# FFT filter and snake MLP on one core: the first DFT stage of batches 3 to 7 by sums and differences on GpSimd, batch 1's forward pieces half a step later, and another order of the last stores

## The chip, the cores and the metric

The kernel runs on one core of a Trainium2 chip. The metric is the time of one execution on the device in microseconds (us). Five engines work side by side, each through its own instructions in order: TensorE (PE in the profile), VectorE (DVE), ScalarE (ACT), GpSimd (POOL) and SyncE (SP), which here only issues DMAs. PEld is TensorE's loading of weights.

## The reference

```python
def _attn_ref(x, filt_r, filt_i):          # x: 8 batches, 3008 rows, 256 channels, float32
    X = np.fft.rfft(x, axis=1)
    F = (filt_r + 1j * filt_i)[None, :, :]
    return np.fft.irfft(X * F, n=x.shape[1], axis=1)

def _moe_ref(x, w_in, w_out, alpha):       # x: 24064 x 256, w_in: 256 x 2048, w_out: 2048 x 256
    h = x @ w_in
    s = np.sin(alpha * h)
    g = h + s * s / (alpha + 1e-09)
    return g @ w_out
```

The second function takes the first one's result as 24064 rows of 256. A filter in frequency over each batch's 3008 rows is followed by two matrix products with an activation between them.

## The kernel before

The transform of length 3008 = 47 x 64 is done in two stages. For each batch from 1 on the class `Spectral` holds the pieces:

- `load_x` (L141, GpSimd's queue): four loads of 94 rows x 8 x 256, fp32 cast to fp16 on the way. Each starts only after the activation that was last recorded (`after(ins, marks["snake"])`).
- `first` (L181): 16 matmuls, 94 rows of contraction (47 samples x 2 halves) by 96 outputs (24 frequencies, real and imaginary part, 2 halves) over 512 columns; `evac` copies the result from PSUM to `t1_h`, two of three times on ACT (L160), else on DVE (L162). After every fourth a store goes from `t1_h` to `d1` in DRAM (L186, SP).
- `load_t2` (L193, GpSimd's queue): eight loads that bring `d1` back turned, 64 rows x 6 x 256 each; two of them make the group of three forward pieces.
- `forward` (L201): 12 pieces of two matmuls of 256 columns; ACT copies to `xf` (L204); two DMAs on SP swap the halves into `xs` (L208).
- `product`, `cross` (L215, L221, L222): the filter, on DVE.
- `inverse` (L232) and the store of `g` to `d2` (L239, SP); `load_t4` (L244, SP); `last` (L254): the inverse's second stage into `y`.

The MLP runs over 48 chunks of 512 (some 384) columns. `hidden` makes 128 hidden units at a time: two matmuls `ph` (L541), a sine on ACT (L545), one operation on DVE (L546). `project` makes 8 matmuls `po` of 256 columns (L558); two tiles of 128 columns are copied by ACT (L566) to `o` and go out by `store` (L586) in parts, since the 94 rows of a run of `y` wrap inside a tile: 4 to 8 DMAs per pair of tiles, on GpSimd's queue up to chunk 4, then on SP. In the last chunk each of the last two tiles is copied and stored by itself, with ACT's queue as the second one.

Batch 0 is done ahead of all this by another path. From there on the order is written out by hand. `put(at, fn, ...)` files each piece under a step; a chunk has eight steps. In a step stand four `ph` matmuls (two hidden blocks), a slot for pieces due, eight `po` matmuls, and a second slot at half a step. A slot lets in one piece with matmuls, more only if it is overdue by over a step:

```python
            if pending[0][2]:
                if run and pending[0][0] > at - 1:
                    break
                run += 1
```

With z = 48 b, batch b's first stage is filed from z - 67 on (0.66 of a step apart), its t2 loads at z - 56, its first forward piece at z - 46.8; in batch 1 the forward pieces begin at step 17.5, 1.25 apart. All engines keep the order in which the pieces are let in, so a piece that waits for data holds up what stands behind it on its engine.

Of the kernel before, what the change touches and what calls it, by code (L numbers as in the profile page):

```python
# [20 lines left out]
N1, N2 = 47, 64  # L21
NS, NQ = 24, 64
NR = 2 * N1
NK = 4 * NS
FUSED = 1


def dft_tables():

    n1, n2 = np.arange(N1), np.arange(N2)  # L30
    s, q = np.arange(NS), np.arange(NQ)
    ph = 2 * np.pi * np.outer(n1, s) / N1
    w = np.stack([np.cos(ph), -np.sin(ph)], 1)
    wf = np.zeros((N1, 2, 2, NS, 2))
    wi = np.zeros((2, NS, 2, N1, 2))
    v = np.stack([2 * np.cos(ph), -2 * np.sin(ph)], 0)
    v[0, :, 0], v[1, :, 0] = 1.0, 0.0
    for h in range(2):
        wf[:, h, :, :, h] = w
        wi[:, :, h, :, h] = v.transpose(0, 2, 1) * (8.0 / S)  # L40

    kap = np.where(q[:, None] < 32, s + N1 * q[:, None], s + N1 * (95 - q[:, None]))
    sg = np.where(q < 32, 1.0, -1.0)[:, None]
    th = 2 * np.pi * n2[:, None, None] * kap / S
    c, sn = np.cos(th), np.sin(th)
    d = np.zeros((2, N2, NS, 2, NQ))
    d[0, :, :, 0] = c.transpose(0, 2, 1)
    d[1, :, :, 0] = sn.transpose(0, 2, 1)
    d[0, :, :, 1] = (-sn * sg).transpose(0, 2, 1)
    d[1, :, :, 1] = (c * sg).transpose(0, 2, 1)  # L50
    f16 = np.float16
    wf, wi = wf.reshape(N1 * 2, 2, NS, 2), 2 * wi.reshape(2, NS, 2, NR)
    wf0, wi0 = np.zeros((96, 2, 2, 32)), np.zeros((2, 2, 32, NR))
    wf0[:NR, :, :, :NS] = wf.transpose(0, 1, 3, 2)
    wi0[:, :, :NS] = wi.transpose(0, 2, 1, 3)
    d = d.reshape(128, NS, 128).astype(f16)
    e = d.transpose(2, 1, 0) * f16(0.125)
    return (wf.reshape(NR, NK).astype(f16), wi.reshape(NK, NR).astype(f16), d,
            wf0.reshape(96, 128).astype(f16), wi0.reshape(128, NR).astype(f16), e)


# [1 line left out]
def kernel(  # L63
# [8 lines left out]
    out: bass.AP,  # L72
):
    nc = tc.nc
    wf_host, wi_host, d_host, wf0_host, wi0_host, e_host = dft_tables()
    wf_dram = nc.inline_tensor(wf_host, name="wf_tbl")
    wi_dram = nc.inline_tensor(wi_host, name="wi_tbl")
    d_dram = nc.inline_tensor(d_host, name="d_tbl")
    wf0_dram = nc.inline_tensor(wf0_host, name="wf0_tbl")
    wi0_dram = nc.inline_tensor(wi0_host, name="wi0_tbl")  # L80
# [13 lines left out]
        return ctx.enter_context(tc.tile_pool(name=name, bufs=bufs, **kw))  # L94

    cpool = pool("consts", 1)
    xpool = pool("xp", 4)
    t2pool = pool("t2", 4)
    xfpool = pool("xf", 3)
    ppool = pool("pp", 4)  # L100
# [7 lines left out]
    ops = pool("ops", 2, PSUM)  # L108

    wf_t = cpool.tile([NR, NK], FP16)  # L110
    t1_h = [cpool.tile([128, 16, C], FP16, name=f"t1_h{i}") for i in range(2)]
    t4_a = cpool.tile([128, 2, 16, C], FP16)
    t4_h = [t4_a[:, i] for i in range(2)]

    def by_half(t):

        return t.rearrange("p a (b c) -> p (a b) c", c=128)

    cos_all = cpool.tile([128, 4, 512], FP32)
    y = cpool.tile([128, 2, 2, 32, NR], FP16)  # L120
# [15 lines left out]
    marks = {}  # L136

    def load_x(b, ch):
        xt = xpool.tile([NR, 8, C], FP16, name=f"x_{b}_{ch}", tag="x")
        for n0, n in [(0, 8)] if b or ch < 3 else [(0, 4), (4, 4)]:  # L140
            ins = nc.gpsimd.dma_start(  # L141
                out=xt[:, n0:n0 + n],
# [14 lines left out]
    def evac(dst, src, on_act=None):  # L157
# [3 lines left out]
        else:  # L161
            marks["dve"] = nc.vector.tensor_copy(out=dst, in_=src)  # L162

    class Spectral:

        def __init__(self, b):
            self.b = b
            self.d1 = dpool.tile([2 * NS, N2, C], FP16, name=f"d1_{b}", tag="d1")
            self.d2 = dpool.tile([2 * NS, N2, C], FP16, name=f"d2_{b}", tag="d2")
            self.d1_rows = self.d1.rearrange("a (h n) c -> (a h) n c", h=2)  # L170
            self.d2_rows = self.d2.rearrange("a (h n) c -> (a h) n c", h=2)
            self.x, self.t2, self.t4, self.xf, self.xs, self.p = {}, {}, {}, {}, {}, {}
            self.fused = b >= FUSED

        def load_x(self, ch):
# [2 lines left out]
        def first(self, i):  # L178
# [6 lines left out]
            if j == 3:  # L185
                nc.sync.dma_start(out=self.d1_rows[:, 8 * ch:8 * ch + 8, :],   # L186
                                  in_=t1_h[ch // 2][0:NK, r0:r0 + 8, :])

        def load_t2(self, g):
            self.t2[g] = t2pool.tile([128, 6, C], FP16, name=f"t2_{self.b}_{g}", tag="t2")  # L190
# [73 lines left out]
    id32 = cpool.tile([16, 16], FP32)  # L264
    nc.scalar.dma_start(out=id32, in_=id32_dram.ap())

    x0 = [xpool.tile([NR, 8, C], FP16, name="x_0_0", tag="x")] + [load_x(0, ch) for ch in range(1, 4)]
    nc.gpsimd.dma_start(out=d_t, in_=d_dram.ap())
    id16 = cpool.tile([128, 128], FP16)
    nc.gpsimd.dma_start(out=id16, in_=id16_dram.ap())  # L270
# [166 lines left out]

    def product_0(i):
        hc, w = blocks[i]
        p0[i] = xpool.tile([128, 2, 4, 128], FP16, name=f"p_0_{i}", tag="x")  # L440
        marks["products"] = nc.vector.tensor_tensor(
            out=p0[i].rearrange("p f s (k c) -> p f s k c", k=2),
            in0=xf0[i].rearrange("p s (k c) -> p s k c", k=2)[:, None].to_broadcast([128, 2, 4, 2, 64]),
# [27 lines left out]
        marks["w_in"] = ins  # L471
    nc.sync.dma_start(out=wf_t, in_=wf_dram.ap())
    nc.sync.dma_start(out=wi_t, in_=wi_dram.ap())
    w_out32 = vpool.tile([128, 16, C], FP32, name="w_out32", tag="v")
    for jb in range(0, 16, 8):
        ins = nc.sync.dma_start(out=w_out32[:, jb:jb + 8],
# [73 lines left out]
    def project(k, u):  # L550

        pb, c0, n = chunks[k]
        t, half = divmod(u, 2)
        final = k == len(chunks) - 1 and t > 1
        if (t % 2 == 0 or final) and half == 0:
            pso[k] = ops.tile([128, 2, C], FP32, name=f"po_{k}_{t}", tag="o")
        for jb in range(8 * half, 8 * half + 8):
# [5 lines left out]
        if half == 1 and (t % 2 == 1 or last or final):  # L563
# [2 lines left out]
            nc.scalar.copy(out=o[:, i0:t % 2 + 1, :], in_=pso[k][:, i0:t % 2 + 1, :])  # L566
            for i in range(i0, t % 2 + 1):
                store(o[:, i, :], pb, c0 + 128 * (t - t % 2 + i),
                      nc.scalar if final else nc.gpsimd if k < 5 or k == len(chunks) - 1 else nc.sync, k < 5)

    def runs(cnt):

        whole = cnt if max(d for d in range(1, 17) if cnt % d == 0) > 7 else cnt - cnt % 16
        return [(0, whole), (whole, cnt - whole)] if 0 < whole < cnt else [(0, cnt)]

    def store(o_blk, pb, col, second, alone):

        p = 0
        queues = [second if alone else nc.sync, second]
        while p < 128:  # L580
            odd, rest = divmod(col + p, S)
            n2, row = divmod(rest, NR)
            cnt = min(128 - p, NR - row)
            t0 = (2 * pb + odd) * S + 32 * row + n2
            for i, (r0, rows) in enumerate(runs(cnt)):
                queues[i].dma_start(  # L586
                    out=bass.AP(tensor=out.tensor, offset=out.offset + (t0 + 32 * r0) * C,
                                ap=[[32 * C, rows], [1, C]]),
                    in_=o_blk[p + r0:p + r0 + rows, :])
            p += cnt  # L590

    pending = []

# [8 lines left out]
    for b in range(1, B):  # L602
        s = s1 if b == 1 else Spectral(b)
        z = 48 * b
        if b > 1:
            for ch in range(4):
                put(22 + 4 * ch if b == 2 else z - 92 + 7 * ch, s.load_x, ch)
        for i in range(16):
            put(6.9 + 0.35 * i if b == 1 else 37 + 0.63 * i if b == 2 else z - 67 + 0.66 * i, s.first, i, pe=True)
        for g in range(4):  # L610
            put(12.5 if b == 1 else 47 if b == 2 else z - 56, s.load_t2, g)
        for u in range(12):
            inv = 23.5 + 1.25 * u if b == 1 else 59 + 2.1 * u if b == 2 else z - 40.8 + 2.3 * u
            fwd = inv - (6 if b == 1 else 6)
            put(fwd, s.forward, u, pe=True)
            put(fwd + (0.5 if b == 1 else 1.5), s.product, u)
            if s.fused:
                put(fwd + (4 if b == 1 else 4.5), s.cross, u)
            put(inv, s.inverse, u, pe=True)
        for ch in range(4):  # L620
            put(z - (9.5 if b == 1 and ch < 3 else (10.5, 10.5, 10.5, 3)[ch]), s.load_t4, ch)
        for u in range(16):
# [60 lines left out]
```

## Time and profile before

| What | Value |
|---|---|
| Time, median of 3 runs | 785.33 us (783.27, 785.33, 3184.2) |
| The profiled execution | 786.9 us, span of its instructions 785.0 us |
| Granted TensorE clock | 1.000 |
| TensorE busy | 773.5 us, 99% of the span |
| DVE, ACT, GpSimd busy | 652.8, 617.7, 113.1 us |
| First stage `first` (L181) | 112 matmuls |
| DMA | 100.99 MB, mean 129 GB/s |

The span is the time from the first to the last instruction; 1.9 us of the profiled execution lie around it. Matmuls overlap, so TensorE's busy time and the mean of one matmul say more than one more matmul costs; the chain of waits gives the time from one start to the next. The columns of a group are: line, engine, operation, output<-inputs, shape, count | busy us, mean ns of one | idle us before them and what ended it. A line of the timeline or of the chain begins with the start and the length in us; a q behind an engine's name is its queue of instructions, which issues DMAs. A line of the waits gives the time in all, how often, and the longest.

### The profile page before, as it was taken

The page shows a single profiled execution, that of the slowest core. Times are in us where ns is not written, and L with a number is a line of the kernel's source. Part 1 is how long each engine was busy: PE and PEld are TensorE (multiplying, and loading weights), DVE is VectorE, ACT ScalarE, POOL GpSimd, SP SyncE. Part 2 cuts the span into 40 slices and gives each one's busy share as a digit, 9 for nine tenths or more (in the row PEclk, how much of TensorE's full clock was granted, in tenths as well). Part 3 has the DMA queues.
Part 4 walks back from the last instruction along what each step waited for, and adds up shares of the span by engine and source line. Part 5 has one row for each costly group of instructions (what it writes and reads, how often), then busy time and mean ns, then how long its engine had stood idle before and what let it go on. Part 6 is the DMA issues. An engine that isn't in the chain of part 4 may idle for free.

```text
span 785.0 us, 16642 instructions
## 1 busy us (share of the span) xinstructions
PE 773.5 (99%) x5799; PEld 535.6 (68%) x5799; DVE 652.8 (83%) x1163; ACT 617.7 (79%) x1213; POOL 113.1 (14%) x190
## 2 busy tenths in 40 slices
PE   8998999999999999999999999999999999999998
PEld 4756767676677666777667776767667776766666
DVE  6886997899878997799878998789987899777773
ACT  5797988888878887888878888788787887777674
POOL 6356544400020000200020000200002000000000
PEclk9999999999999999999999999999999999999999
DMA  9955586665664546654574454835456233421111
GB/s 215 276 111 153 115 184 193 155 127 121 171 166 85 129 104 194 145 124 107 128 210 107 104 115 131 227 87 124 114 159 177 65 98 78 119 62 28 41 41 54
DMA packets 86655, 100.99 MB, mean 129 GB/s; under 512 B 14896, under 2 KB 74294, under 8 KB 86572
## 3 DMA queue, kind: packets, MB, share of 16 engines
q1 hardware_dynamic: 74644, 71.11, 32.7%
q0 software_dynamic: 11712, 28.78, 18.5%
q8 instruction: 45, 0.74, 0.4%
q14 instruction: 38, 0.31, 0.1%
q10 hardware_dynamic: 216, 0.05, 0.0%
HBM read 55.72 MB, written 46.66 MB: 130 GB/s over the span
## 4 chain that ended last, share of the span: by engine, by line
PE 93%; DVE 3%; DMA 2%; ACT 1%; issue 1%; SPq 0%; POOL 0%; ACTq 0%; DVEq 0%; POOLq 0%
PE po L558 40%; PE ph L541 40%; PE pa L181 3%; PE pb L201 2%; PE pd L254 2%; PE pc L232 2%; DVE v L546 1%; PE pc L453 1%; DMA al<-in_moe_alpha_dram 1%; PE warm L377 1%; DMA d<-t_h 1%; PE pb L431 1%; DMA t<-d 0%; PE pa L399 0%; SPq L586 0%
## 5 line engine op out<-in xcount | busy, mean ns | idle before, releaser
L546 DVE SCALAR_TENSOR_TENSOR v<-cos_all,ph 128x512 f16<-128x512 f32 (+1 forms) x768 | 483.1, 671 | 110.9 <-ACT cos_all L545 107.7
L545 ACT ACTIVATE cos_all<-ph 128x512 f32<-128x512 f32 (+1 forms) x768 | 411.2, 592 | 94.1 <-PE ph L541 93.2
L558 PE MATMUL po<-w,v 128*128 128x256 f16 x3008 | 389.3, 272 | 0.0
L541 PE MATMUL ph<-y,w 128*128 128x512 f16 (+1 forms) x1536 | 387.8, 374 | 0.7 <-DVE v L546 0.6
L558 PEld LDWEIGHTS <-v 128*128 128x128 f16 x3008 | 288.3, 98 | 77.9 <-issue 1.5
L541 PEld LDWEIGHTS <-w 128*128 128x128 f16 x1536 | 147.9, 98 | 103.8 <-issue 3.3
L566 ACT COPY o<-po 128x512 f32<-128x512 f32 (+1 forms) x97 | 55.7, 574 | 20.7 <-PE po L558 14.3
L586 POOL DMA_DIRECT2D out_dram<-o x67 | 34.8, 528 | 208.3 <-ACT o L566 207.4
L204 ACT CAST xf<-pb 128x512 f16<-128x512 f32 x84 | 49.9, 594 | 14.7 <-PE pb L201 13.1
L193 POOL DMA_DIRECT2D t<-d x56 | 36.3, 663 | 172.7 <-DMA out_dram<-o 96.7
L141 POOL DMA_DIRECT2D x<-in_x_dram x32 | 17.2, 539 | 266.6 <-PE pc L232 160.0
L160 ACT CAST t_h<-pa 96x512 f16<-96x512 f32 x77 | 45.0, 584 | 8.4 <-PE pa L181 8.2
L160 ACT CAST y<-pd 128x376 f16<-128x376 f32 (+1 forms) x83 | 39.9, 480 | 8.2 <-PE pd L254 4.4
L254 PEld LDWEIGHTS <-t_a 96*128 96x128 f16 x448 | 31.4, 97 | 18.6 <-issue 0.4
L181 PE MATMUL pa<-x,wf_t 94*96 94x512 f16 x112 | 42.5, 381 | 0.7 <-ACT t_h L160 0.4
L160 ACT CAST g<-pc 128x512 f16<-128x512 f32 x59 | 35.0, 594 | 7.4 <-PE pc L232 7.0
L222 DVE TENSOR_TENSOR p<-p,xs 128x512 f16<-128x512 f16 x84 | 35.7, 425 | 2.9
L254 PE MATMUL pd<-wi_t,t_a 96*128 96x94 f16 x448 | 37.1, 204 | 0.0
L221 DVE TENSOR_TENSOR xs<-xs,filt_t 128x512 f16<-128x512 f16 x84 | 35.1, 417 | 0.0
L215 DVE TENSOR_TENSOR p<-xf,filt_t 128x512 f16<-128x512 f16 x84 | 35.0, 417 | 0.0
L201 PE MATMUL pb<-t,d_t 128*128 128x256 f16 x168 | 32.0, 272 | 2.1 <-DMA t<-d 2.0
L232 PE MATMUL pc<-p,e_t 128*128 128x256 f16 x168 | 32.1, 273 | 0.0
(64 smaller groups left out, 285.0 us busy)
## 6 DMA issues: line engine op xcount, KB each, us to landing
x<-in_x_dram POOLq DMA_DIRECT2D x30, 376.0 KB, 4.9
d<-t_h SPq DMA_DIRECT2D x28, 384.0 KB
t<-d POOLq DMA_DIRECT2D x56, 192.0 KB, 4.5
xs<-xf SPq DMA_DIRECT2D x168, 64.0 KB
d<-g SPq DMA_DIRECT2D x56, 192.0 KB
t_a<-d SPq DMA_DIRECT2D x28, 384.0 KB
out_dram<-o SPq DMA_DIRECT2D x92, 80.0 KB
w_out<-in_moe_w_out_dram SPq DMA_DIRECT2D x2, 1024.0 KB
```

The costliest lines, as they stand in the source:

```text
L160: marks["act"] = nc.scalar.copy(out=dst, in_=src)
L181: marks["pe"] = nc.tensor.matmul(out=ps[0:NK, :], lhsT=wf_t, rhs=self.x[ch][:, 2 * j:2 * j + 2, :], start=True, stop=True)
L193: nc.gpsimd.dma_start(out=self.t2[g][64 * p:64 * p + 64, :, :], in_=self.d1[a0:a0 + 6, :, :].rearrange("s n c -> n s c"))
L201: nc.tensor.matmul(out=ps[:, i, :], lhsT=d_t[:, s, :], rhs=self.t2[s // 6][:, s % 6, :], start=True, stop=True)
L204: nc.scalar.copy(out=self.xf[u], in_=ps)
L232: nc.tensor.matmul(out=ps[:, i, :], lhsT=e_t[:, 2 * w + i, :], rhs=pt[:, i, :], start=(k == 0), stop=(k == len(pr) - 1))
L254: nc.tensor.matmul(out=psv[:, i, :], rhs=wi_t, start=True, stop=True, lhsT=t4_h[ch // 2][0:NK, n0 % 16 + i, cb * 128:cb * 128 + 128])
L541: nc.tensor.matmul(out=ps[:, 0:n], lhsT=w1[:, cb, jb * 128:jb * 128 + 128], rhs=y_cols[:, cb, c0:c0 + n], start=(cb == 0), stop=(cb == 1))
L545: nc.scalar.activation(out=cs[:, 0:n], in_=ps[:, 0:n], func=AFT.Sin, bias=float(np.pi / 2))
L546: marks["snake"] = nc.vector.scalar_tensor_tensor(out=v[k][:, jb, 0:n], in0=cs[:, 0:n], scalar=-1.0, in1=ps[:, 0:n], op0=ALU.add, op1=ALU. ...
L558: nc.tensor.matmul(out=pso[k][:, t % 2, :], lhsT=v[k][:, jb, 128 * t:128 * t + 128], rhs=w2[:, jb, :], start=(jb == 0), stop=(jb == 15))
L566: nc.scalar.copy(out=o[:, i0:t % 2 + 1, :], in_=pso[k][:, i0:t % 2 + 1, :])
```

## The change

Batches 3 to 7 (`FOLDED = 3`) use the symmetry of the cosine and the sine: the samples k and 47 - k of the 47 are first added and subtracted, and then one matmul over 24 sums gives the real parts, another over 24 differences the imaginary ones. Five rows of 13 places each stand side by side on 120 partitions (5 x 13 = 65 for the 64 places; the first is a dummy), so that 13 places of 256 channels are done for each part.

- 15 loads per batch (`load_mirror`) in place of four: seven pairs of 115 rows x 2 (once 1) x 256, and one of 5 rows x 13 x 256.
- `fold`, seven times: GpSimd writes the sum to a free corner of `t1_a` or `x_all`, then the difference in place of the first operand; 120 x 512, the last time 120 x 256.
- `first_folded`, seven times two matmuls with the table `wp_t` (120 x 120 for each part), 512 columns, the last pair 256; 13 evacuations. The stores to `d1` come after the fourth and the last fold, each in two halves (real, imaginary) on SP.
- The first stage is now filed from z - 62.3 on (batch 3: z - 61), 1.38 steps per fold, the folds up to 3.4 steps ahead of it, the t2 loads at z - 52.4 (batch 3: z - 51.5). The forward pieces stay where they were.
- The x buffers become one tile, as do the two `t1_h`; the table `wp` is one more load on SP before `w_out`.
- Batch 1's forward pieces begin at step 18 and stand 1.21 apart. In the other batches the cross of pieces 10 and 11 comes half a step earlier and the inverse of piece 11 comes 0.9 steps later.
- The last two tiles of the last chunk change places, and their parts go, the largest first, to SP, ACT and GpSimd in turn.

```diff
+FOLDED = 3
+NJ, NL = 5, 13
+NF = NJ * NS
...
+    even = np.cos(ph[:NS])
+    odd = -np.sin(ph[:NS])
+    wp = np.einsum("kis,jm->jiksm", np.stack([even, odd]), np.eye(NJ))
+    wp = np.concatenate([wp[:, 1:].reshape(NF - NJ, 2, NF), wp[:, 0].reshape(NJ, 2, NF)])
...
-    t1_h = [cpool.tile([128, 16, C], FP16, name=f"t1_h{i}") for i in range(2)]
+    t1_a = cpool.tile([128, 2, 16, C], FP16)
+    t1_h = [t1_a[:, i] for i in range(2)]
+    wp_t = cpool.tile([NF, 2, NF], FP16)
...
+    x_all = cpool.tile([128, 4, 8, C], FP16)
...
+    STORES = {3: 0, 6: 8}
+    NP = (NL + 1) // 2
+    x_rows = x_all.rearrange("p a n c -> p (a n) c")
+    mirror = [x_rows[:, 16 * k:16 * k + NL, :] for k in range(2)]
+    sums = [t[0:NF, NL:NL + 2, :] for t in (t1_h[0], t1_h[1], x_rows[:, 0:16], x_rows[:, 16:32])]
+
+    def start_folding():
+
+        nc.gpsimd.memset(mirror[1].bitcast(UINT32), 0)
...
+        def load_mirror(self, k, l0, n):
+            rows = [mirror[k][0:NF - NJ, l0:l0 + n]] + ([] if k or l0 else [mirror[k][NF - NJ:NF]])
+            for at, t in zip((N2 * (N1 - 1) if k else N2, 0), rows):
+                run = n if at else NL
+                ins = nc.gpsimd.dma_start(
+                    out=t, in_=bass.AP(tensor=x.tensor, offset=x.offset + (self.b * S + at - 1 + l0) * C,
+                                       ap=[[NL * C, NJ], [-N2 * C if k else N2 * C, NS - 1 if at else 1],
+                                           [1, run * C]]))
+                after(ins, marks["snake"])
+
+        def fold(self, i):
+            l0, n = 2 * i, min(2, NL - 2 * i)
+            xa, xb = [t[0:NF, l0:l0 + n, :] for t in mirror]
+            self.e[i] = sums[i % 4]
+            after(nc.gpsimd.tensor_tensor(out=self.e[i][:, 0:n, :], in0=xa, in1=xb, op=ALU.add), marks["snake"])
+            nc.gpsimd.tensor_tensor(out=xa, in0=xa, in1=xb, op=ALU.subtract)
+
+        def first_folded(self, i, k):
...
+            nc.tensor.matmul(out=dst, lhsT=wp_t[:, k, :], rhs=src, start=True, stop=True)
+            if n == 2:
+                evac(t1_a[0:NF, k, l0:l0 + 2, :], ps[0:NF])
+            elif k == 1:
+                evac(t1_a[0:NF, :, l0, :], ps[0:NF])
+            if i in STORES and k == 1:
+                lo = STORES[i]
+                n = l0 + n - lo
+                for part in range(2):
+                    nc.sync.dma_start(out=self.d1_fold[part, :, lo:lo + n, :], in_=t1_a[0:NF, part, lo:lo + n, :])
...
+        if final:
+            t = 5 - t
...
-                      nc.scalar if final else nc.gpsimd if k < 5 or k == len(chunks) - 1 else nc.sync, k < 5)
+                      (nc.sync, nc.scalar, nc.gpsimd) if final else (nc.gpsimd,) if k < 5 else
+                      (nc.sync, nc.gpsimd) if k == len(chunks) - 1 else (nc.sync,))
...
+        if len(queues) == 3:
+            parts = [(i, *part[1:]) for i, part in enumerate(sorted(parts, key=lambda part: -part[1]))]
...
+        if s.folded:
+            if b == FOLDED:
+                put(z - 94, start_folding)
+            for i in range(NP):
+                for k in range(2):
+                    put(z - 92 + 2.6 * i + 1.3 * k, s.load_mirror, k, 2 * i, min(2, NL - 2 * i))
+            for i in range(NP):
+                at = z - (61 if b == 3 else 62.3) + 1.38 * i
+                put(max(at - 3.4, z - (62.6 if b == 3 else 64.6)), s.fold, i)
+                for k in range(2):
+                    put(at + 0.7 * k, s.first_folded, i, k, pe=True)
...
-            put(12.5 if b == 1 else 47 if b == 2 else z - 56, s.load_t2, g)
+            put(12.5 if b == 1 else 47 if b == 2 else z - (51.5 if b == 3 else 52.4), s.load_t2, g)
...
-            inv = 23.5 + 1.25 * u if b == 1 else 59 + 2.1 * u if b == 2 else z - 40.8 + 2.3 * u
+            inv = 24 + 1.21 * u if b == 1 else 59 + 2.1 * u if b == 2 else z - 40.8 + 2.3 * u
...
-                put(fwd + (4 if b == 1 else 4.5), s.cross, u)
-            put(inv, s.inverse, u, pe=True)
+                put(fwd + (4 if b == 1 or u > 9 else 4.5), s.cross, u)
+            put(inv + (0.9 if b > 1 and u == 11 else 0), s.inverse, u, pe=True)
```

## The prediction

> **What bounds the kernel now.** I read the page first, then TensorE's list of waits, the chain of waits around the moved pieces, and the timeline of the queues between the first DFT stage and the second.
>
> From the page:
>
> ```profile
> PE 773.5 (99%) x5799; PEld 535.6 (68%) x5799; DVE 652.8 (83%) x1163; ACT 617.7 (79%) x1213; POOL 113.1 (14%) x190
> ...
> PE 93%; DVE 3%; DMA 2%; ACT 1%; issue 1%; SPq 0%; POOL 0%; ACTq 0%; DVEq 0%; POOLq 0%
> ...
> L181 PE MATMUL pa<-x,wf_t 94*96 94x512 f16 x112 | 42.5, 381 | 0.7 <-ACT t_h L160 0.4 <-ACT y L160 0.2
> ```
>
> TensorE works through the whole span and 93% of the chain lies on it; the granted clock is 1.00. GpSimd is busy for 14%. The 381 ns of a matmul contain overlap with the next; the chain gives the price of one more. From the chain of waits:
>
> ```profile
> 310.53 0.87 PE po L558 x8
> 311.40 0.17 PE pd L254 x4
> 311.57 0.65 PE ph L541 x4
> ...
> 320.52 0.88 PE po L558 x8
> 321.39 1.73 PE ph L541 x8
> 323.12 0.17 PE pd L254 x4
> 323.29 0.88 PE po L558 x8
> 324.16 0.22 PE pb L201 x2
> ```
>
> Eight matmuls of 256 columns take 0.87, so 0.109 each, and one of 512 columns 0.217. TensorE's waits hold one that matters:
>
> ```profile
> PE pb L201 <- DMA t<-d: 2.0, 1, 2.0
> ```
>
> It is the first forward piece of batch 1 at 73.24. After 75 us TensorE waits for nothing (the list of its waits from 75 to 770 is empty), so from there on time is gained only by fewer columns, and every new wait of TensorE counts in full.
>
> **What is gained.** (a) A folded batch does 12 matmuls of 512 and 2 of 256 columns in place of 16 of 512: 3 x 0.217 = 0.65 us, five times 3.2 us. (b) The first forward piece of batch 1 moves from 17.5 behind the four hidden matmuls of step 18 (0.87) with four pieces of the last stage between them (0.04 each): 1.0 of the 2.0 us is filled with work, and 1.0 of waiting stays. (c) At the end TensorE finishes at 781.3; the copy follows, then SP issues two stores one after the other (0.32 and 0.46) and ACT two. Now the last tile has three parts, one on each queue: one issue of about 0.4 less, of which I take 0.3, since GpSimd's store lands 1.9 to 2.1 us after its issue like the others; between 0 and 0.5. Together 4.5 us.
>
> **What GpSimd takes on.** Per folded batch 15 loads in place of 4 (0.54 each: 6 us more) and 14 sums and differences, all in GpSimd's own order. No row has an f16 sum there. From GpSimd's groups by form, and VectorE's for the same kind:
>
> ```profile
> L482 POOL TENSOR_TENSOR w<-w_in,y 128x512 f16<-128x512 f32 x2 | 2.6, 1287 | 0.0
> ...
> L514 POOL TENSOR_TENSOR w<-w_out,rec_t 128x1024 f16<-128x1024 f32 x3 | 5.6, 1896 | 0.0
> ...
> L222 DVE TENSOR_TENSOR p<-p,xs 128x512 f16<-128x512 f16 x84 | 35.7, 425 | 2.9
> ```
>
> The bounds are 0.43 (VectorE's f16 row) and 1.90 (a row of twice the width); I take 1.29, the same shape on the same engine. A batch then needs 12 x 1.29 + 2 x 0.73 + 14 gaps of 0.1 = 18.3 us. In the instruction order of the changed kernel fold 0 may start some 3.9 us before TensorE's first folded matmul, and the last one follows 18.7 us later: 22.6 us of cover. Nothing waits, with 4.3 us to spare; the break-even is 1.62 us per operation. [...]
>
> The other loads and edits I cost at nothing, with their cover: the x loads land in 4.9 us and are issued ten steps ahead of the folds; the one table on SP (0.36 to 0.63) delays w_out, first read at 43.6, while SP is done with it at 31.8; the moved cross and inverse of piece 11 leave 6 us of the 8 between the d2 stores (295.9) and the t4 loads behind them (304.0); ACT and DVE lose three evacuations per batch off the path; the one memset falls into idle time of GpSimd. Without its cover the table would cost 0.5 us, the inverse 1.7 per batch.
>
> **What is lost.** The first stage now ends about four steps nearer to the second. Between them lies a chain: last matmul, evacuation, store of d1 (SP), load of t2 (GpSimd, it waits for the store), first forward matmul. Timeline around batch 4, SP, GpSimd, TensorE:
>
> ```profile
> 307.10 0.38 PE L181 MATMUL pa<-x,wf_t 94*96 94x512 f16 x1
> ...
> 309.49 0.30 SPq L186 DMA_DIRECT2D d<-t_h  x1
> ...
> 313.77 5.17 POOL L193 DMA_DIRECT2D t<-d  x8 [32.29 <-DMA out_dram<-o]
> ...
> 315.44 2.41 SPq L586 DMA_DIRECT2D out_dram<-o  x6
> ...
> 324.00 0.38 PE L201 MATMUL pb<-t,d_t 128*128 128x256 f16 x2
> ```
>
> GpSimd's load starts 4.28 after SP's store starts; two loads of 0.66 make the first group, and the second of them lands 3.56 after its start: store to data 8.5 us. For batches 1 to 7 I get 9.0, 8.1, 9.7, 8.5, 9.0, 9.9, 9.2; mean 9.0, and 0.1 until TensorE runs. Before, TensorE had 16.9 us of other work in between (19.5 in odd batches). That the rows priced above add up to 16.87 for the same stretch says the sum can be trusted for the new order. There, from the last folded matmul to the first forward one, it gives 8.4 us in batch 3, 9.5 in 4 and 6, 11.2 in 5 and 7.
>
> To this comes what stands before the store on SP. In batches 4 to 7 the matmul now follows directly on the one that completes an output pair, and that pair's stores precede the d1 store on SP: 0.9 to the end of ACT's copy, then 2.4 for six stores (the line at 315.44) or 1.5 for four: store start 3.4 us after the matmul in batches 4 and 6, 2.5 in 5 and 7. In batch 3 only the evacuation lies before it (rows: 1.0 to 2.4; I take 1.4). The store is in two halves of 300 KB instead of one of 384, the second issued 0.3 later, as its load is issued 0.66 later: no change.
>
> Waits of TensorE: batch 3: 1.4 + 9.1 - 8.4 = 2.1. Batches 4 and 6: 3.4 + 9.1 - 9.5 = 3.0 each. Batches 5 and 7: 2.5 + 9.1 - 11.2 = 0.4 each. Sum 8.9. With the shortest row (8.1) it is 5.0, with the longest (9.9, and 2.4 for the evacuation) 14.4. During the wait everything behind the piece on TensorE's queue stands still, hidden matmuls included, and VectorE and ACT run dry; TensorE can't win it back.
>
> [...]
>
> **Sum.** -4.5 + 8.9 = +4.4 us. The profiled execution took 786.9 (span 785.0 and 1.9 around it): 791.3. The median of the runs is 1.6 lower, 785.3, so I forecast 789.7.
>
> **Rivals.** *The chain closes in time* (chance 0.27). For it: in batch 2 today the data land 0.25 us before the forward piece without a wait, with a chain of 8.1; the new stores are shorter and fewer large loads run beside them. Against it: batches 4 and 6 would need store to data in 6.0, which no row shows. Time: 785.3 - 4.5 = 780.8; with 1 us of remaining waits 782.
>
> *GpSimd too slow* (0.06, the slower side): if an f16 operation takes over 1.62 us, TensorE waits at the folded matmuls, last at number 6. At the 1.90 of L514 a batch needs 26.3 us, 3.7 over the cover, five times 18.5: 789.7 + 18.5 = 808. For it: two SBUF operands and an in-place difference that must wait for its sum. Against it: both shapes of L482 (1.29 for 512, 1.84 for 768 columns) lie near 2.2 ns per column plus 0.15, and VectorE's L546 ran beside them at its usual 0.68.
>
> *The wait of batch 1 moves along* to the next piece, since the data come no earlier: 1.0 more, 790.7; inside the range.
>
> **How the numbers follow.** My case has 0.63: 785.8 to 795.2 with its own bounds. The first rival holds 0.27 and pulls the low end to 779.5 (780.8 less 0.2 for the full gain at the end, and part of the 2 us by which the runs shown differ). The GpSimd case stays outside, the third rival inside; 0.04 is left for what I have not seen. A measurement of this kernel tells about 2% from no change, 15.7 us: faster than 769.6 needs more than the whole gain (0.01), slower than 801 needs the GpSimd case (0.05 with a little of its 0.06 falling short), within 0.94.
>
> **What would show it.** Right: L249, 70 matmuls, chain price 0.217; the folds at 1.2 to 1.4 us and no wait of the folded matmuls for POOL; among TensorE's waits pb <- DMA t<-d six times, about 1.0 for batch 1, 2 for batch 3, 3 for batches 4 and 6, little for 5 and 7; d1's second stores behind six or four out stores on SP. Wrong: an empty list of waits after 75 us (the first rival), or waits for POOL at the folded matmuls (the second), or operations of L546 longer than 0.68 during the folds.

## The result and the profile after

The changed kernel takes 790.22 us, the median of seven runs (788.25 to 793.96), beside 784.49 for the kernel before on the same chip: the ratio is 1.0077, with a 95% interval from 1.0057 to 1.0096. By the 2% that a measurement of this kernel tells from no change that is "the same"; by the interval it is a real loss of some 6 us. Run again beside other experiments it took 791.86 (ratio 1.0086, 1.0056 to 1.0116). The change costs 5.7 us by the first measurement and 6.8 by the second; the forecast was 4.4. The profiled execution took 790.22, its span is 788.1 and its mean granted clock 0.998.

From the page of the changed kernel:

```profile
PE 770.7 (98%) x5789; PEld 534.0 (68%) x5789; DVE 649.2 (82%) x1158; ACT 614.2 (78%) x1203; POOL 227.8 (29%) x318
...
PE 86%; DMA 5%; DVE 4%; issue 2%; ACT 1%; POOL 0%; SPq 0%; POOLq 0%; ACTq 0%; DVEq 0%
...
L236 POOL TENSOR_TENSOR t_a<-x_all 120x512 f16<-120x512 f16 x20 | 23.0, 1152 | 97.2 <-DVE v L618 97.1
```

TensorE has ten matmuls fewer and is busy for 2.8 us less. But its share of the chain fell from 93% to 86%, and DMA's rose from 2% to 5%: the end now hangs on transfers at some places. GpSimd's busy time doubled; a sum took 1.15 us. TensorE's list of waits from 75 to 770 us, empty before, now reads:

```profile
PE pb L272 <- DMA t<-d: 5.1, 4, 2.2
PE pc L303 <- DVE p L293: 0.7, 1, 0.7
PE pb L272 <- DVE v L618: 0.2, 1, 0.2
```

`pb` is the first forward piece of a batch, waiting for t2. No folded matmul (L249) waits for POOL. The timeline around batch 4, the same place as in the prediction:

```profile
312.82 0.27 PE L249 MATMUL pa<-x_all,wp_t 120*120 120x256 f16 x1
...
313.63 2.41 SPq L664 DMA_DIRECT2D out_dram<-o  x6
316.14 0.83 SPq L258 DMA_DIRECT2D d<-t_a  x2
...
319.26 0.71 POOL L264 DMA_DIRECT2D t<-d  x1 [12.01 <-DMA d<-t_a]
...
320.44 4.56 POOL L264 DMA_DIRECT2D t<-d  x7 [0.47 <-DMA d<-t_a]
...
324.00 0.39 PE L272 MATMUL pb<-t,d_t 128*128 128x256 f16 x2 [1.53 <-DMA t<-d]
```

The last folded matmul starts at 312.82, the store stands behind six out stores on SP, as forecast, and starts 3.32 later, the first load 3.12 after that, and TensorE goes on 7.86 us after the store began, having waited 1.53. The chain of waits of the same stretch shows the two transfers as links of the path that sets the end:

```profile
316.61 3.55 DMA d<-t_a
320.15 0.28 issue
320.44 3.52 DMA t<-d
323.96 0.05 issue
324.00 0.39 PE pb L272 x2
```

And one thing that no step of the prediction held. After batch 6's wait of 2.2 us the granted clock fell. Three stretches of 3.41 us, with TensorE's busy time, matmuls, granted clock, DMA share and GB/s:

```profile
509.36:512.78 3.42, 1.25 (x9) 1.00 0.99 270
512.78:516.19 3.41, 3.41 (x15) 0.50 1.02 215
516.19:519.60 3.41, 3.41 (x30) 1.00 0.13 29
```

In the second stretch TensorE did 15 matmuls, in the third 30. Half speed for 3.41 us costs 1.7. Going by the mean clock, not every execution has it: the six profiles of this document with such a fall have 0.997 or 0.998, the eight without 0.999 or 1.000. Of the seven runs three show a mean clock of 0.997 or 0.998 and took 790.22, 792.9 and 793.96 us; the four at 1.000 took 788.25 to 790.22.

**Where the 3.1 us between the two spans (785.0 and 788.1) went.** I took the times at which the same hidden matmuls start in both traces and compared what lies between them with the work by the chain's prices (0.216 for 512 columns, 0.109 for 256); what is over is time lost.

| Stretch | After against before, us |
|---|---|
| Start-up until the first `ph` matmul of the chunks | -1.67 |
| Steps 16 to 48 (batches 1 and 2) | -1.47 |
| Steps 48 to 336: work, five times 0.65 | -3.25 |
| Steps 48 to 336: gaps ahead of the first forward pieces (1.26, 1.69, 0, 2.33, 0.48) | +5.76 |
| the clock at 0.5 for 3.41 us | +1.7 |
| batch 3's inverse, whose product waits for `xs` | +0.9 |
| smaller gaps, together | +0.9 |
| The end, after the last matmul | +0.28 |

The start-up ends between 35.9 and 38.0 us in the 14 profiles, whatever the kernel, so the -1.67 of this pair is chance. The -1.47 can't be credited to the change either: steps 16 to 48 take 65.7 to 67.2 us in the three profiles with batch 1 filed as before and 65.4 to 67.4 in the eleven with it filed as in the change, in the mean 66.3 in both. Without these two the pair differs by 6.2 us, near the 5.7 and 6.8 between the medians.

### The profile page after: what moved, and what is told of

It reads as the page before. It is cut to its first block, busy times and chain, and to the rows that moved or that the text cites. A ratio compares the mean times of both kernels' runs of the same rounds, so it can differ in the third digit from the quotient of the medians.

```text
span 788.1 us, 16837 instructions
## 1 busy us (share of the span) xinstructions
PE 770.7 (98%) x5789; PEld 534.0 (68%) x5789; DVE 649.2 (82%) x1158; ACT 614.2 (78%) x1203; POOL 227.8 (29%) x318
## 4 chain that ended last, share of the span: by engine, by line
PE 86%; DMA 5%; DVE 4%; issue 2%; ACT 1%; POOL 0%; SPq 0%; POOLq 0%; ACTq 0%; DVEq 0%
PE po L632 37%; PE ph L613 37%; DVE v L618 2%; PE pb L272 2%; PE pc L303 2%; DMA t<-d 2%; PE pd L325 2%; DMA d<-t_a 2%; PE pa L249 2%; PE pa L214 1%; PE pc L524 1%; DMA xs<-xf 1%; DMA cos_all<-in_x_dram 1%; PE warm L448 1%; ACT cos_all L617 1%
## 5 line engine op out<-in xcount | busy, mean ns | idle before, releaser
L618 DVE SCALAR_TENSOR_TENSOR v<-cos_all,ph 128x512 f16<-128x512 f32 (+1 forms) x768 | 482.2, 671 | 115.5 <-ACT cos_all L617 112.9
L664 POOL DMA_DIRECT2D out_dram<-o x69 | 35.9, 527 | 203.9 <-ACT o L640 202.6
L226 POOL DMA_DIRECT2D x_all<-in_x_dram x75 | 47.5, 635 | 149.2 <-DVE v L618 143.1
L236 POOL TENSOR_TENSOR t_a<-x_all 120x512 f16<-120x512 f16 x20 | 23.0, 1152 | 97.2 <-DVE v L618 97.1
L177 ACT CAST t_a<-pa 120x512 f16<-120x512 f32 (+1 forms) x67 | 39.5, 590 | 9.5 <-PE pa L249 5.6
L325 PEld LDWEIGHTS <-t_a 96*128 96x128 f16 x448 | 31.5, 97 | 21.9 <-issue 2.0
L237 POOL TENSOR_TENSOR x_all<-x_all 120x512 f16<-120x512 f16 (+1 forms) x35 | 38.0, 1085 | 2.7
L293 DVE TENSOR_TENSOR p<-p,xs 128x512 f16<-128x512 f16 x84 | 35.7, 425 | 2.9
L292 DVE TENSOR_TENSOR xs<-xs,filt_t 128x512 f16<-128x512 f16 x84 | 35.0, 417 | 3.2 <-DMA xs<-xf 3.2
L325 PE MATMUL pd<-wi_t,t_a 96*128 96x94 f16 x448 | 37.2, 204 | 0.2
```

The source lines that it names most:

```text
L177: marks["act"] = nc.scalar.copy(out=dst, in_=src)
L226: ins = nc.gpsimd.dma_start(out=t, in_=bass.AP(tensor=x.tensor, offset=x.offset + (self.b * S + at - 1 + l0) * C, ap=[[NL * C, NJ], [-N2 * ...
L237: nc.gpsimd.tensor_tensor(out=xa, in0=xa, in1=xb, op=ALU.subtract)
L325: nc.tensor.matmul(out=psv[:, i, :], rhs=wi_t, start=True, stop=True, lhsT=t4_h[ch // 2][0:NK, n0 % 16 + i, cb * 128:cb * 128 + 128])
L618: marks["snake"] = nc.vector.scalar_tensor_tensor(out=v[k][:, jb, 0:n], in0=cs[:, 0:n], scalar=-1.0, in1=ps[:, 0:n], op0=ALU.add, op1=ALU. ...
```

## The experiments

All times are medians beside the kernel before run on the same chip, which took 784.40, 784.43, 784.67 and 785.05 us in the four sets.

**The small parts alone.** The kernel before, with batch 1's forward pieces and the last stores as in the changed kernel:

```diff
-            inv = 23.5 + 1.25 * u if b == 1 else ...
+            inv = 24 + 1.21 * u if b == 1 else ...
...
```

> The kernel before with batch 1's later forward pieces and the new order of the last stores, without folding. Theory (the folded batches' gain and loss lie elsewhere): batch 1's wait for t2 falls from 2.0 us to 1.0 or less, and the stretch from TensorE's last matmul to the end, 3.71 us before and 3.99 in the changed kernel, is again 4.0; no other wait. Time 783 to 784 against 784.5, no granted clock below 1.000 after the start. Rival (the small parts carry part of the loss): 785 or more.

Measured: 784.73 us, ratio 1.0005 (0.9994 to 1.0015). Its waits hold

```profile
PE pb L201 <- DMA t<-d: 1.0, 1, 1.0
...
PE pd L343 <- ACT xf L204: 0.4, 1, 0.4
```

The wait of 2.0 became 1.0, as worked out, but a piece of the last stage now waits 0.4 for ACT, and the end is longer by 0.36. The time lies above the 783 to 784 expected and is level with the kernel before.

**The stage later, without sums.** The kernel before with nothing but its first stage of batches 3 to 7 filed where the changed kernel has it:

```diff
-                    else z - 67 + 0.66 * i, s.first, ...
+                    else z - (61.9 if b == 3 else 63.2) + 0.66 * i, s.first, ...
-            put(... else z - 56, s.load_t2, g)
+            put(... else z - (51.5 if b == 3 else 52.4), s.load_t2, g)
```

> The kernel before, its plain first stage filed 3.8 steps later (batch 3: 5.1), so that its last matmul and its last store stand where the changed kernel's stand: 8.5, 9.6, 11.3, 9.6, 11.3 us of TensorE work to the first forward piece in batches 3 to 7, the same out stores ahead on SP. No sums on GpSimd, no extra loads. Theory (distance between the stages): TensorE waits at the first forward piece as in the changed kernel, about 1 us in batch 3, 1.5 to 2.5 in 4 and 6, little in 5 and 7, sum 4 to 7; time 788.5 to 793, with a granted clock below 1.000 in some runs. Rival (GpSimd's sums or the 15 loads make the wait): no such waits, 784.5.

Measured: 789.92 us, ratio 1.0062 (1.0047 to 1.0076).

```profile
PE pb L201 <- DMA t<-d: 4.0, 4, 2.0
```

The distance alone makes a loss of 5.5 us, with no operation on GpSimd and no fewer columns. After batch 4's wait of 2.0 us the clock fell to 0.5 here too, for 3.41 us. It is most of what the changed kernel lost, but not all. By the count of the table above TensorE lost 6.7 us in steps 48 to 336 here and 9.2 in the changed kernel. Of the 2.5 between them 1.1 are longer waits at the forward pieces and 0.9 is batch 3's inverse, which does not wait in every profile of the changed kernel.

**Out stores ahead of the d1 store.** The changed kernel with the second pair of stores to d1 on ACT's queue, where no out stores stand ahead:

```diff
-                    nc.sync.dma_start(out=self.d1_fold[part, ...
+                    (nc.scalar if i == 6 else nc.sync).dma_start(out=self.d1_fold[part, ...
```

> The changed kernel with the second pair of d1 stores of each folded batch issued from ACT's queue in place of SP's, so that they no longer stand behind four or six out stores. Theory: the store starts some 2 us earlier after the last folded matmul in batches 4 and 6 and 1 us in 5 and 7; the waits of batches 4, 6 and 7 go (under 0.5 each), the one of batch 3, whose store stood behind nothing, stays near 1 us. Time 782 to 785. Rival (the landing of the transfers, not SP's order, makes the wait): the waits of 4 and 6 stay above 1 us, time 788 or more.

Measured: 788.80 us, ratio 1.0058 (1.0041 to 1.0074).

```profile
PE pb L272 <- DMA t<-d: 4.7, 4, 2.1
```

TensorE lost 1.08 and 1.23 us ahead of the forward pieces of batches 4 and 6 (1.69 and 2.33 in the changed kernel), and nothing in batch 7 (0.48), but 2.27 in batch 3 and 0.80 in batch 2. In batches 4 and 6 the store started 1.1 to 1.3 us after the last matmul instead of 3.3, but the forward matmul came 9.3 and 9.6 us after the store's start instead of 7.9 and 8.5. So taking the store past the queue won 0.5 to 1.1 us a batch in this pair of profiles, and the two transfers themselves are most of the chain. The time is the one that the rival had forecast.

**The folded stage two steps earlier.**

```diff
-                at = z - (61 if b == 3 else 62.3) + 1.38 * i
-                put(max(at - 3.4, z - (62.6 if b == 3 else 64.6)), s.fold, i)
+                at = z - (63 if b == 3 else 64.3) + 1.38 * i
+                put(max(at - 3.4, z - (64.6 if b == 3 else 66.6)), s.fold, i)
...
-            put(... else z - (51.5 if b == 3 else 52.4), s.load_t2, g)
+            put(... else z - (53.5 if b == 3 else 54.4), s.load_t2, g)
```

> The changed kernel with the folds, the folded matmuls and the t2 loads of batches 3 to 7 two steps earlier: 13.1 to 15.9 us of TensorE work between the last folded matmul and the first forward piece. Theory (distance): no wait of TensorE for t2 in batches 3 to 7, the gain of 3.2 us for fewer columns and 1 to 2 for batch 1 remain, time 779.5 to 782, clock 1.000 in all runs. Rival (folding costs by itself, or GpSimd and DVE collide since the last crosses of the batch before now overlap with the folds): 785 or more, with waits for POOL or for DVE.

Measured: 787.51 us (784.48 to 789.89), ratio 1.0033 (1.0019 to 1.0047). No forward piece of batches 3 to 7 waited any more, but the gain expected did not come. Its profile lost 3.5 us more in the first 16 steps than the kernel before, where ACT waited for the weights `w_out`, and the clock then was 0.5 for 3.41 us:

```profile
47.02 0.91 ACT L584 ACTIVATE w<-w_out,rec_t 128x256 f16<-128x256 f32 x2 [1.76 <-DMA w_out<-in_moe_w_out_dram]
```

Steps 48 to 336 took 556.6 us, 0.2 more than in the kernel before, so gaps of TensorE took back the 3.2 us there too; the largest part of them, 2.0, lies ahead of folded matmuls.

**The table behind w_out.** That asked whether the new table `wp_t`, loaded by SP ahead of `w_out`, is to blame. In the changed kernel:

```diff
-    nc.sync.dma_start(out=wp_t, in_=wp_dram.ap())
...
+    nc.sync.dma_start(out=wp_t, in_=wp_dram.ap())
```

> The changed kernel with one move: the load of the 56 KB table wp_t stands on SP's queue behind the two loads of w_out, not ahead of them. In the profile of fold_early ScalarE waited 1.8 us for w_out in the start-up (the two loads of w_out were issued at 29.8 and 30.4 us, the table at 28.7), and TensorE then lost 3.5 us up to its 16th step, 1.7 of it by a clock of 0.5. Theory (the table's issue of some 0.5 us makes w_out late in a part of the runs, and it is in the changed kernel's median too): median 788.3 to 789.3 beside the 790.2 of the changed kernel, and no run over 791. Rival (the table costs nothing, the late w_out was chance): 789.7 to 790.7, runs up to 793 as before. The waits of the forward pieces stay in both, 4 to 5 us in all.

Measured: 792.48 us, ratio 1.0099 (1.0077 to 1.0121): not faster. The same move in fold_early:

> fold_early (sums, folded matmuls and loads of t2 two steps earlier) with the table behind w_out. Theory one (start-up lost what the earlier stage won): median 785.0 to 786.0 beside the 787.5 of fold_early, with no wait for w_out. Theory two, on top of it: VectorE's f16 products L292 and L293 that run beside GpSimd's sums take 1.26 to 1.41 us, not 0.42 (5 of 84 in fold_early's profile), and make the first folded matmuls of batch 3 wait 1.0 us for VectorE's eviction; these stay here, so the median stays over 784. Rival (no start-up effect): 787 to 788.

Measured: 786.06 us (785.37 to 787.71), ratio 1.0017 (1.0006 to 1.0028), 1.45 us less. The two pairs speak against each other. What this profile did show was the second cost that its expectation named. Its timeline near the first sums of batch 3:

```profile
194.66 1.15 POOL L236 TENSOR_TENSOR t_a<-x_all 120x512 f16<-120x512 f16 x1 [18.84 <-DVE v L618]
195.88 1.15 POOL L237 TENSOR_TENSOR x_all<-x_all 120x512 f16<-120x512 f16 x1
195.90 1.42 DVE L292 TENSOR_TENSOR xs<-xs,filt_t 128x512 f16<-128x512 f16 x1
...
197.00 1.33 POOL L236 TENSOR_TENSOR t_a<-x_all 120x512 f16<-120x512 f16 x1
197.35 1.26 DVE L293 TENSOR_TENSOR p<-p,xs 128x512 f16<-128x512 f16 x1
...
200.46 0.43 PE L249 MATMUL pa<-t_a,wp_t 120*120 120x512 f16 x1 [1.05 <-DVE t_a L179]
```

Beside a sum, VectorE's f16 sum L293 takes 1.26 us in place of 0.42 (all 5 that overlap a sum, of 84; the other 79 take 0.42 to 0.43). Of five L292 beside a sum two take 0.92 and 1.42; the three that start in the last 0.13 us of one sum, ahead of the next, keep 0.42. Ten of GpSimd's operations stretch from 1.15 to between 1.22 and 1.34. VectorE's eviction is then late, and a folded matmul waits 1.05. In the changed kernel none of these products overlaps a sum: its sums begin at z - 64.6, and the last cross product of the batch before is filed at z - 65.5. Two steps earlier they collide. So the sums can't simply follow the matmuls forward. VectorE's L618, which takes one operand from PSUM, stays at 0.67 to 0.69 us beside the sums.

**Sums in place, matmuls closer together.** The sums stay where the changed kernel has them; the matmuls of a batch take 14.5 to 16.2 us from the first to the last, in place of 18.7 to 20.0, so that the last one comes earlier by 1.6 to 2 steps. The table stands behind w_out:

```diff
-                at = z - (61 if b == 3 else 62.3) + 1.38 * i
+                at = z - (61 if b == 3 else 62.6) + 1.12 * i
...
-                    put(at + 0.7 * k, s.first_folded, i, k, pe=True)
+                    put(at + 0.6 * k, s.first_folded, i, k, pe=True)
...
-            put(... else z - (51.5 if b == 3 else 52.4), s.load_t2, g)
+            put(... else z - (53.1 if b == 3 else 54.4), s.load_t2, g)
```

> The changed kernel with the table behind w_out, the sums at their steps of the changed kernel, and the folded matmuls closer together (1.12 steps a pair, not 1.38), so that the last one of a batch and the loads of t2 come 1.7 to 2 steps earlier (batch 3: 1.6); TensorE's work between the last folded matmul and the first forward piece is 12.3 to 15.9 us, as in fold_early, not 8.4 to 11.2. The sums then lie behind the last cross product of the batch before. Theory (two things cost: the short distance, and sums beside VectorE's f16 products): no forward piece of batches 3 to 7 waits over 0.3 us, L292 and L293 stay at 0.42 us, folded matmuls wait under 0.5 us in all; 781.0 to 783.0, that is 1.4 to 3.4 below the kernel before: 3.2 for the columns, 1.0 for batch 1, less some small losses and 0.3 at the end. Rival (the evictions, 14 in 14.5 us instead of 18.7, are late beside the activations, and TensorE waits for them): 784 to 786, with waits of L249 or of ph for ScalarE or VectorE of 2 us and more.

Measured: 787.12 us, ratio 1.0038 (1.0022 to 1.0053). No forward piece of batches 3 to 7 waits, L292 and L293 are at 0.42 throughout, as expected; but the time missed by 4 us, by a wait that neither theory had. From 150 us on:

```profile
PE pd L325 <- DMA t_a<-d: 2.2, 3, 1.0
PE pc L303 <- DVE p L293: 1.1, 2, 0.6
```

L325 is the last stage of the batch before; it waits for t4. SP's timeline in batch 4 shows why:

```profile
298.35 2.76 SPq L664 DMA_DIRECT2D out_dram<-o  x7
303.20 0.78 SPq L258 DMA_DIRECT2D d<-t_a  x2
304.07 3.27 SPq L315 DMA_DIRECT2D t_a<-d  x3
```

The first pair of stores to d1 is now filed at z - 58.6, ahead of the loads of t4 at z - 58.5. SP is free at 301.1, but it holds the store until the folded matmuls are evacuated at 303.2, and t4's loads stand behind it.

**t4 ahead of that store.** One step earlier for the loads of t4 in fold_tight; the last stores are again those of the kernel before (edit not shown):

```diff
-            put(z - (9.5 if b == 1 and ch < 3 else (10.5, 10.5, 10.5, 3)[ch]), s.load_t4, ch)
+            put(z - (9.5 if b == 1 and ch < 3 else (11.5, 11.5, 11.5, 3)[ch]), s.load_t4, ch)
```

> fold_tight with two moves: the loads of t4 (for the last stage of the batch before) are filed one step earlier, so that on SP's queue three of them stand ahead of the first pair of d1 stores, not behind it; and the last tile's stores are those of the kernel before. In fold_tight's profile TensorE lost 0.76, 0.30, 1.12 and 0.81 us to t4's loads (pd L325 for DMA), which stood behind a store that waits for the folded stage. Theory (that order on SP is what fold_tight lost, beside small waits of products and of batch 2): these 3.0 us go and the end gives 0.3, so 787.1 becomes 783.5 to 784.3, level with the kernel before. Rival (t4's data is late by itself, not by its place in the queue): 786.3 to 787, with the waits of L325 still there.

Measured: 782.67 us (781.59 to 785.79), ratio 0.9974 (0.9963 to 0.9986): 2.0 us under the kernel before, and 7.6 and 9.2 under the changed kernel's two medians. The interval lies below 1, though 2.0 us are less than the 2%; the time is 0.8 below the range expected. SP's timeline and, in a fence of its own, all of TensorE's waits from 150 us on:

```profile
298.02 2.39 SPq L658 DMA_DIRECT2D out_dram<-o  x6
300.51 1.25 SPq L315 DMA_DIRECT2D t_a<-d  x3
302.50 0.78 SPq L258 DMA_DIRECT2D d<-t_a  x2
```

```profile
PE pc L303 <- DVE p L293: 0.3, 1, 0.3
```

The loads go at 300.5, as in the changed kernel, and the 3.0 us are gone. Between the medians lie 4.5; the end accounts for 0.3 of them, and the waits of L303 fell by 0.8. Steps 48 to 336 take 554.4 us, 2.0 less than in the kernel before. The larger waits that are left lie in batches 1 (1.2) and 2 (0.5). So batch 2 was tried:

```diff
-                put(6.9 + 0.35 * i if b == 1 else 37 + 0.63 * i, s.first, i, pe=True)
+                put(6.9 + 0.35 * i if b == 1 else 36 + 0.63 * i, s.first, i, pe=True)
```

> tight_t4, and batch 2's first stage one step earlier (from step 36, not 37). In fold_tight's profile the first forward piece of batch 2 lost 1.26 us (in the kernel before its data lands 0.25 us ahead of need). Theory (no slack there, and the stores' completion differs by 1 us and more from run to run): 0.5 to 1.0 under tight_t4, 782.8 to 783.6, a little faster than the kernel before (784.4). Rival: no difference to tight_t4.

Measured: 783.45 us, ratio 0.9979 (0.9960 to 0.9998): no gain. In its profile batch 2's forward piece waits no more, but the batch's first stage now loses 1.03 us ahead of two of its matmuls.

**Filing t2 later.** To see when the clock falls, the kernel before got its loads of t2 later:

```diff
-            put(... else z - 56, s.load_t2, g)
+            put(... else z - 56 + (0, 0, 0, 4.8, 4.1, 6.2, 5.0, 6.6)[b], s.load_t2, g)
```

> The kernel before with only its loads of t2 filed later: 4.8, 4.1, 6.2, 5.0 and 6.6 steps in batches 3 to 7. By the slack of 8.3, 6.0, 9.0, 5.6 and 7.8 us that the profile of before shows between t2's landing and the first forward piece, the waits should be some 1, 2, 3, 4 and 5 us. It asks when the granted clock falls. Theory (a wait of about 2 us can be enough, depending on how it lies to a fixed beat of 3.4 us, one of 4 us always is): no fall after the wait of 1 us, one after each of 4 and 5 us, each a stretch of 3.4 us at 0.5, which costs 1.7 us; 2 and 3 us open. Time 784.4 + 15 + 1.7 times 2 to 4, so 803 to 806. Rival (the fall in the changed kernel had another cause than the wait): no fall at all, 799 to 800.

Measured: 784.31 us, ratio 0.9999 (0.9986 to 1.0013), and no new wait at all. The experiment missed its aim: in batch 4 the load started 4.23 us after the store, before 4.28. GpSimd reaches the load early and waits for the store in both; a later step changes its place in GpSimd's order but not what it waits for. So the steps of t2's loads decide nothing here; the store does. The change and the edits above move them too. What a forward piece's wait of 4 us or more does to the clock is not shown.

**Repeats.** The table ahead of w_out again, in the best version, and the changed kernel once more:

> tight_t4 with the table wp_t loaded ahead of w_out, as in the changed kernel. It asks for the table's place where no other wait covers it: fold_early lost 1.45 us to fold_early_table, but the changed kernel was 2.3 us better than table_later. Theory (the table ahead makes w_out late in a part of the runs): 1.0 to 2.0 over tight_t4's 782.7, so 783.7 to 784.7, with more spread upwards. Rival (its place is worth nothing, both differences were the spread between runs): 782.2 to 783.2.

Measured: 783.93 us (781.15 to 788.84), ratio 0.9979 (0.9957 to 1.0001). Its profile has the same wait of 1.76 us for w_out and lost 3.3 us at the start-up, but the interval covers tight_t4's ratio.

> The changed kernel once more, unaltered, to see how far its median holds: 790.22 us of 7 runs, from 788.25 to 793.96, and table_later 792.48. If the table's place costs nothing, the two belong to one spread, and this gives between 790 and 792.5 with runs up to 794 to 796; if the later table makes it slower, 789.5 to 790.5. In the profile: waits of the forward pieces of batches 3, 4, 6 and 7, and a clock of 0.5 for 3.4 us after each stretch of 3.413 us (counted from the first fall or rise of the clock) in which TensorE stood still for over 2.05 us, after none with under 2.0.

Measured: 791.86 us (790.38 to 794.89). With this, table_later's 792.48 lies in the changed kernel's spread. In the profile the clock fell once, after a stretch of 3.413 us with 2.16 us idle, and not after one with 1.97, as expected. Of the ten profiles of kernels with sums, w_out is late in two of the five with the table ahead and in none of the five with it behind. That w_out is late in some executions, and that this costs some 3.4 us, is shown; that the table's place is the cause, or what it is worth on the median, is not. One sign points to it: in the two late profiles SP issued the second load of w_out at 30.4 and 31.7 us, in the twelve others at 27.0 to 29.6.

## Why the prediction was right, and where its steps were off

The forecast was 789.7, measured were 790.2 and 791.9. The sign, the mechanism and the total hold; late_no_fold shows the mechanism by itself, and fold_tight and tight_t4 show it by taking the wait away. That the total is so near is in part luck: a term too large was made up by terms that were missing, and the kernel before took 784.5, not the 785.3 that the forecast starts from, so the loss forecast was 4.4 and the loss measured 5.7 and 6.8.

- **Fewer columns, -3.2 us: right.** TensorE's work between the same steps is 92.34 to 92.51 us a batch, 92.99 to 93.16 before. tight_t4, where little takes it back, keeps 2.0 of it.
- **Batch 1, -1.0 us: worth nothing that can be measured.** The 2.0 us that the step started from belong to one execution. In the 14 profiles the load of t2 starts either 3.6 to 3.7 us (8 times) or 4.7 to 5.2 us (6 times) after batch 1's last store. Filed as before, TensorE then waits 0.6 to 0.8 or 2.0; filed as in the change, 0 or 0.8 to 1.3. So the wait does get shorter, but the stretch around it does not: steps 16 to 48 take 66.3 us in the mean either way, and small_parts as a whole is level. The third rival, that the wait moves along to the next piece, is not what happens: small_parts has one wait for t2, of 1.0.
- **The end, -0.3 us: the wrong sign.** From the last matmul to the end of the span it is 3.99 us, 3.71 before. GpSimd, which was idle at the end before, issues its store 0.70 after the last matmul and drains until 3.13; SP's own drain follows at 3.16, in the kernel before at 2.88. In small_parts SP drains at 2.79 and GpSimd only at 3.29, and the end comes at 4.07: there it is GpSimd that the others wait for. All eight profiles with the new order have 3.97 to 4.07, the six with the old one 3.65 to 3.72. The step counted issues, but the end follows the last drain of a queue that held a store: by 0.83 in the changed kernel and in the kernel before, by 0.78 in small_parts.
- **GpSimd, 1.29 us an operation: 1.15 measured**, within the bounds, and no wait, as forecast. The rival "GpSimd too slow" falls. What the step did not ask is what the sums do to VectorE; in the changed kernel nothing, by their place.
- **The waits, 8.9 us: the mechanism right, the size too large.** The prediction had 2.1, 3.0, 0.4, 3.0, 0.4 for batches 3 to 7; the list of waits has 1.1, 1.5, 0, 2.2, 0.3, in sum 5.1 (the table's count from start to start adds some 0.16 to each), and changed_again 1.0, 2.0, 0, 2.1, 0, again 5.1. The delay on SP was worked out well (3.3 after the matmul in batches 4 and 6, forecast 3.4; 2.4 in 5 and 7, forecast 2.5). The term that failed is the time from the start of the store to the forward matmul, set at 9.1: it is 8.3, 7.9, 8.5 and 9.3 in batches 3, 4, 6 and 7, so under it in the three batches that mattered (batch 5 did not wait). The seven rows come from stores at the old place. That the new ones are smaller is not the reason: late_no_fold, with stores as before at the new place, has 7.7, 8.4 and 7.8 in batches 3, 4 and 6. In the changed kernel the first load starts 3.0 to 3.6 us after the store's start (4.0 to 5.6 before), and the first two loads are there 4.7 to 5.7 later (4.0 to 4.8 before). Why the load follows the store sooner at the new place is not shown.
- **Missing terms.** The clock after a wait (+1.7 in the executions that have it), batch 3's product late for its inverse (+0.9 in this profile, nothing in changed_again's), and smaller gaps (+0.9). Gap by gap TensorE lost 9.2 us more than before in steps 48 to 336, where the prediction had 8.9.
- **"The table would cost 0.5 us without its cover", 0 with it: left open.** SP is done with the issues of w_out before 34 us in all profiles, but in fold_early part of the data was there only at 47.0, where ACT had been ready for it at 45.3. The step took the end of the issue for the landing.
- **The first rival**, the chain closes in time, falls for this kernel: it needed 6.0 us from store to data in batches 4 and 6, and they took 7.8 and 8.4. Its 780.8 is about what tight_t4 reaches (782.7), by ending the stage earlier.

## What to carry to other kernels

When one engine works without a gap, a stage moved nearer to the next is paid for by the time of the transfers between them, plus what stands ahead of the store in its queue. Here it was 7.7 to 9.7 us from the start of the store to the matmul that waited, with one store of 384 KB or two of 300. To move work earlier, look at what each of its parts runs into: the sums ran into VectorE's two-operand products (0.92 to 1.42 us in place of 0.42 in fold_early_table), and an earlier store held up the loads behind it on a queue that keeps its order (3.0 us in fold_tight). And the step at which a load is filed said nothing here, since it waited for a store anyway; look at what a load waits for.

## What the runs showed of the hardware

- **The clock fell after idle time within fixed stretches.** In every trace the granted clock changes at whole multiples of 3.413 us after its first change; in the changed kernel's the fall comes 508.59 us after it, 149 times 3.4133. I summed TensorE's idle time in each such stretch, gap by gap: from the start of one matmul to the start of the next, less the chain's price of the first. From the start of the chunks to the last matmul the clock fell six times, each time after a stretch with 2.08 to 2.28 us idle (fold_early, table_ahead, table_later, late_no_fold and both runs of the changed kernel), and never after one with up to 2.01. The line between the two depends on this count: by the profile's busy time, in which a matmul's end is modelled, the stretches ahead of a fall have 1.6 to 2.2 us idle and others up to 2.0. A single gap need not do it: in table_later 2.35 us of waiting in batch 6 lay across the border of two stretches, 2.01 of it in the one, and nothing fell. Each fall lasted one stretch of 3.41 us.
- **A load starts early or late after the same store.** Behind the same store of batch 1 the load started 3.56 to 3.72 us after the store's start in eight profiles and 4.68 to 5.22 after it in six, in kernels of all kinds. Batch 2's store, at its own place in 13 profiles, shows no such two groups, but the same spread: 4.0 to 5.3. From these spreads, of 1.7 and 1.3 us, I estimate that in this kernel a stage whose data lands with less than 1.5 us to spare can wait in some executions.
- **VectorE and GpSimd.** In fold_early_table the seven f16 operations of VectorE on two SBUF operands that start in the first half of a GpSimd sum take 0.92 to 1.42 us in place of 0.42; the three that start in its last 0.13 us keep 0.42. L618, which reads PSUM, stays at 0.67 to 0.69.
